# Attention and FFN in one kernel: ScalarE's Exp passes alternately two and three PSUM banks wide

## The chip, the cores and the metric

The kernel runs on one core of one Trainium2 chip. The metric is the device time of one execution in microseconds (us), as the median of the runs shown. A core has five engines with their own instruction queues, each running in order: TensorE (PE in the profile; its weight loads are PEld), VectorE (DVE), ScalarE (ACT), GpSimd (POOL) and SyncE (SP, which here only starts transfers). Matmul results land in PSUM. The kernel uses it as eight banks of 128 partitions by 512 float32 columns.

## The reference

For one sequence of S = 2048 tokens with D = 512 features, an attention block with 32 heads of width 16 and a SwiGLU FFN of inner width 1792 are computed from the same x, and mixed by a gate:

```python
g = sigmoid((x * gate_w).sum(-1, keepdims=True))
q, k, v = split_heads(x @ A_wqkv)                  # 32 heads of 16
p = softmax(q @ k.T * 16 ** -0.5)                  # 2048 x 2048 per head
a = merge_heads(p @ v) @ A_wo
b = (silu(x @ B_w_gate) * (x @ B_w_up)) @ B_w_down
out = g * a + (1 - g) * b
```

Inputs and output are bf16. The 32 x 2048 x 2048 = 134 million exponentials are the largest single item.

## The kernel before, in words

**Tiling.** Queries come in 4 blocks of 512 columns (`QB`, `QBW`), heads in 8 groups of four (`G`), keys in 16 tiles of 128 (`KT`). A *unit* is one query block with one head group; there are 32 (`UNITS`). A unit and a key tile make a *tile* of scores: four *blocks*, one for each head, of 128 keys by 512 queries. There are 512 tiles and 2048 blocks.

**Two ways to the exponential.** A tile goes one of two ways as a whole.
- On ScalarE: `emit_pair` (line 774) takes two blocks, has TensorE write their scores into `s_t`, a PSUM tile of two banks, and has ScalarE run one Exp over all 1024 columns into the SBUF tile `e_t` (line 793). Four blocks take two passes. Two `s_t` tiles exist, so one is filled while the other is read. Ten `e_t` buffers exist (`EB`).
- On VectorE and GpSimd: `emit_d` (line 855) writes one block into `d_t`, a single *shared* bank. VectorE turns the scores into the bits of an exponential with one TENSOR_SCALAR from PSUM to SBUF (`c_t<-d_t`; some tiles use spare space in `kaug` or `wd_t` instead). Then a tile is finished either with four shifted copies or with two masks and a product (`quad`, `groups`); VectorE runs these passes, and GpSimd takes strips of the columns of many of them.

Afterwards `pv` (line 1104) multiplies the exponentials by V into `o_ps`, one bank, accumulated over the whole unit. A column of ones in V also gives the softmax denominators.

**How score matmuls share TensorE.** A head's scores need only 32 of TensorE's 128 rows, so several blocks run side by side on different rows in one round. A `d_t` block *rides* along in the round of a pair, on the rows of heads that the pair does not use.

**PSUM.** Two `s_t` tiles (4 banks, `ps_s`), `o_ps` (1 bank, `ps_o`), and 3 shared banks (`ps_m`). The shared banks serve `d_t` and all other products: projections (`qp`, `kp`, `vp`), the FFN's `gu`, the output products `ops` and `dps`. A bank is taken by `m_tile` (line 396) and comes free once VectorE has emptied it (`m_free`).

**Order.** The whole program is straight-line; a planner fixes the order of the instructions while it is built. It keeps its own clocks for TensorE, VectorE, ScalarE and GpSimd (`plan.pe`, `plan.dve`, `plan.act`, `plan.pool`) with a price for each operation (`ACT_US` = 0.9167 for an Exp pass) and the times at which it expects the shared banks to be free (`banks`). The main loop (lines 1754 to 1814) fills the time until the next `s_t` tile is free with `pv` products or pieces of projections and FFN (`Chain`, `Pacer`, ordered by deadline), then emits the next pair. Where more than 0.4 us is left, it adds a filler product on `o_ps` with zero weights (line 1799). `want_d` (line 1741) says how many `d_t` blocks ride: at most as many as shared banks that the planner expects to be open at that moment, less one if another chain needs it:

```python
open_ = sum(b is not None and b <= max(plan.pe, s_end[pairs[0] % 2]) + (BANK_WAIT if way_of(pairs[0]) != "x" else 0.5) for b in banks)
...
return max(0, min(2, open_ - int(one), (3 if way_of(pairs[0]) != "y" else 4) - len(d_wait)))
```

`v_unit` (line 1700) chooses the unit whose last ScalarE tile is handed to VectorE instead. So how many tiles each engine gets is not written down; it comes out of these rules. On top of the rules, `TURNS` (line 88) is a string with two characters for each pass, read by `turn_of` and `way_of`: a letter at a place nudges one decision there.

**FFN.** Gate and up products of one 128-wide chunk are two chains of four pieces. `gate` (line 715) puts a Tanh, `th`, into ScalarE's queue between the passes; two VectorE passes follow. The weights of a chunk are loaded three chunks ahead into four buffers (`w_load`, `ffnw`).

**Head and tail.** Ahead of the loop, the first queries and six key tiles are projected and bounded (lines 1282 to 1366); the other ten key tiles follow under the first passes, and the queries are then computed again with the final bound (`q0_again`). After the loop the last unit's `o_ps` is copied in halves by ScalarE and VectorE, its denominators are inverted and spread over the rows, and four output tiles are finished with the last products of the output projection (`tail`, lines 1252 to 1268 and 1854 to 1887).

Of the kernel before, what the change touches and what calls it, by code (L numbers as in the profile page):

```python
# [54 lines left out]
class Pacer:  # L55
# [27 lines left out]

TURNS = (
    ".......u................g.a.k...............i...a................n.....x...v..s................."
    "j............x.x....e....g.......r.r.g....c.c...a......x..................e....r.w.....y........"  # L90
    "......hn.x..............j.h.........if.....v.......m........k.............i....q..........a....."
    "....h.o..........r.........f..f.h.........gt.....uhm............................................"
    "....................j................................qb..g.r.............x.................y...."
    "........k.d............g.f......f..o...............w................hf................k..t...r.."
    "..........s.........h........w...f........................s............................g........"
    ".......g.......v...y...r........k......o........c..............................................."
    ".....d..........i.a......lo..g......e..t..e..v.......r.........................................."
    "............a..m....f...i.k......rk........x.......lk.............k..........d...............g.."
    "..............b....y........o......w.....u..e..f.................r....b........................."
    "........................e................................u...m.........v..i........w.qcq.....w.."  # L100
    "bm.q..e.......c.......................................a..................u...w.w.......r..g....."
    ".................g.....................................................n..........h............."
    ".......wj.h...k....d.................................l....g......y......ov.n....i......l......k."
    ".n.........ls.g...i.......j.d....lb"
)
# [3 lines left out]
def kernel(  # L109
# [67 lines left out]
    ps_m = [ctx.enter_context(tc.tile_pool(name=f"ps_m{i}", bufs=1, space=bass.MemoryType.PSUM)) for i in range(3)]  # L177
# [150 lines left out]
    banks = [0.0] * 3  # L328
    held = [None] * 3
# [66 lines left out]
    def m_tile(name, ride=None):  # L396
        while m_ready() is None:
            stuck()
        i = min((i for i in range(3) if banks[i] is not None), key=lambda i: banks[i])
# [359 lines left out]
    def score(ps, b, rows=64):  # L759
# [3 lines left out]
        q = (q0a if n < FT else q0[qb])[r, j % 2, :] if g == 0 else get_q(qb, g)[r, j % 2, :]  # L763
        mm(ps, lhsT=kaug[r, g, kt * P:(kt + 1) * P], rhs=q, start=True, stop=True,
           tile_position=(r.start, 0))
# [8 lines left out]
    def emit_pair(bs, ride=0):  # L774
        i = pairs[0] % 2
        plan.pe = max(plan.pe + (FLIP if plan.mode != "R" else 0.0), s_end[i])
        if FT <= bs[0] // 4 < KT:
# [25 lines left out]

    def turn_of(n):

        return TURNS[2 * n] if 2 * n < len(TURNS) else "."

    def way_of(n):

        return TURNS[2 * n + 1] if 2 * n + 1 < len(TURNS) else "."  # L810

    exps = []
    ACT_US = 0.9167
# [9 lines left out]
    def d_slots(half=None):  # L823

        left = vcur["left"] if vcur else range(NV)
        return [k for k in left if half is None or k // 2 == half]
# [341 lines left out]
    def post(un):  # L1168
# [83 lines left out]
    def tail_ready():  # L1252
        for c in list(pace.chains):
            force(c)
        while owed:
            pay()
        assert here_done and len(scaled) == TQ
        al = ps_s.tile([P, 2 * QBW], F32, tag="s", name="al")
        a_ps.append(al)

    def tail(n):

        for _ in range(n):
            tq, i = rest.pop(0)
            if tq == 3 and i == 0:
                a_ps.append(ps_o.tile([P, QBW], F32, tag="o", name="al_o"))
            w, r = last_rows(tq)(i)
            mm(a_ps[tq][:, 0:D], lhsT=w, rhs=r, start=(i == 0), stop=False)

# [14 lines left out]
    def keep_warm(n):  # L1284
        for _ in range(n):
            mm(warm[:, :], lhsT=idle[:, 0:P], rhs=idle[:, :], start=True, stop=True)
# [27 lines left out]
    keep_warm(9)  # L1314
    for i0, i1, h in ((0, TQ, fore), (TQ, FT, aft)):
        for dc in (DC - 1, DC - 2):
            spare_s = dc < DC - 1 and i0
            p = ps_s.tile([P, 2 * QBW], F32, tag="s", name="tp") if spare_s else m_tile("tp")
# [6 lines left out]
            if not spare_s:  # L1325
                m_free(p, 0.0 if dc == DC - 1 else 0.1)
    pad(0)
    keep_warm(1)
    kpf = ps_s.tile([P, 2 * QBW], F32, tag="s", name="kp0")
# [19 lines left out]
    vp0 = m_tile("vp")  # L1349
    v0(vp0, 0, 0, 3)  # L1350
    for p, h in zip(qps, halves):
        bound_add(p[:, 0:HQ], kneg1, aq0[:, h])
    v0(vp0, 0, 3, FT)
# [11 lines left out]
    vec.tensor_copy(**v0_out(vp0, 0, FT))  # L1365
    m_free(vp0, plan.pe + 2.0)

    plan.act = plan.pe
    plan.dve = plan.pe + 2.3
# [7 lines left out]
    def k0_pieces(i, k0, w):  # L1377
# [14 lines left out]
        return columns(DC, "kp", lambda dc: wpad[1][:, dc, :], lambda dc: xT[:, dc, k0:k0 + w], end, c0)  # L1392

# [21 lines left out]
    def scale_part(p):  # L1415
        def f():
# [6 lines left out]
                        1, -101)  # L1423
    second = [pace.add(k0_pieces(2 + i, k0, min(QBW, S - k0)), 1, -100 + 0.1 * i)
              for i, k0 in enumerate(range(FK, S, QBW))]
    for a, c in zip([qp_again] + second, second):
        c.hold = lambda a=a: plan.pe >= 2.3 and a.out()
# [67 lines left out]
    def first_loads():  # L1495
        for i in range(3):
# [7 lines left out]
    for pos, qb in enumerate(ORDER):  # L1504
        a0 = f0 + per * pos
        gus = []
        for i in range(FC * pos, FC * pos + FC):
            gate_pcs, up_pcs = gu_chain(i)

            def first(f=gate_pcs[0][1], i=i):  # L1510
                w_load(i + 3, True)
                w_load(i + 3, False)
# [73 lines left out]
    def pv_list(now):  # L1586

        un = closed
        if un == UNITS or not o_ready(now):
            return []  # L1590
        early = un == 0 and pvs[0] < FT
# [16 lines left out]
    def emit_pv(item, most=QBW):  # L1608
        nonlocal closed
        un = closed  # L1610
        pv(item[0], item[1] if len(item) > 1 else None, most)
# [80 lines left out]
    LEAD, LAST = 8.0, 6.0  # L1692
    TILE_US = 1.9
# [6 lines left out]
    def v_unit():  # L1700
# [4 lines left out]
        while vu < UNITS:  # L1705
# [4 lines left out]
            left = hi[vu] - (at_ + max(half, begun) if vu == au else 0)  # L1710
            if vu >= au and left > 0 and (vu or hi[0] > FT):
# [41 lines left out]

    while au < UNITS:
# [10 lines left out]
        if room > 0.02:  # L1765
# [29 lines left out]
            if room > 0.4 and closed in o_of and 0 < pvs[closed] and pv_left(closed) > 1 and (closed or pvs[0] != FT) and sum(  # L1795
# [13 lines left out]
        begun = 1  # L1809
        emit_pair([4 * n + 2 * half, 4 * n + 2 * half + 1], want_d())  # L1810
        half ^= 1
        begun = 0
        at_ += not half
        forward()
    flush_act()
    while closed < UNITS or vops or vcur:
# [13 lines left out]
        if closed == UNITS - 1 and pv_left(closed) <= 2 and not a_ps[2:]:  # L1830
            tail_ready()
        if len(a_ps) > 2 and not pv_list(plan.pe) and not vops and len(rest) > 1:
            n = closed * KT + done_a[closed]
            if plan.pe + 0.22 < max(e_end.get(b, 0.0) for b in range(4 * n, 4 * n + 4)):
                tail(1)
                spend("F", 1)
                continue
        next_pv()
    for c in list(pace.chains):
# [5 lines left out]
    for n in sorted(at):  # L1845
        for f in at.pop(n):
            f()
    while jobs:
        oust()
    while owed:  # L1850
        pay()
    assert not vops and not vready and not vcur and not d_wait and not copies and au == closed == UNITS


    assert not at
    un = UNITS - 1
    osb = osbs[un]
    tail(min(2, len(rest)))
    dt = m_tile("dt")
    denominators(dt, osb)  # L1860
    rt = work.tile([P, 4 * TQ], BF16, tag="rt", name="rt")
    recip16(rt[:, :], dt[:, 0:4 * TQ])
    tail(sum(r[0] == 2 for r in rest))
    spread_rows(dt, rt, (0,), P)
# [54 lines left out]
```

## Time and profile before

| what | value |
|---|---|
| median of the runs | 743.07 us (2 runs, 742.9 to 743.23) |
| profiled execution: its own time | 742.59 us |
| its span, first to last instruction | 740.9 us |
| granted TensorE clock | 0.999 |
| matmuls; VectorE; ScalarE; GpSimd instructions | 9224; 1227; 827; 362 |
| Exp passes of 1024 columns | 754 |
| `th` passes of 512 columns | 56 |
| `d_t` blocks (into `c_t`, `kaug` and `wd_t`) | 468 + 60 + 12 = 540 |

Columns of a row of instruction groups: line, engine, operation, output<-input, shapes, count, then after the bar the busy time in us, the mean length of one instruction in ns, and the idle time of that engine just before them with what ended it. Instructions of one engine may overlap, so busy time is less than count times mean. A row of the table by stage has the stretch, its length, and each engine's busy time with the number of instructions.

### The profile page before, as it was taken

Reading aid. Unit: us, or ns where it says so; the run is one execution under the profiler, and the core shown is the slowest. Engines: PE = TensorE matmul, PEld = TensorE weight load, DVE = VectorE, ACT = ScalarE, POOL = GpSimd, SP = SyncE. Lnnn points to the kernel's source line nnn. Section 1 sums busy time; section 2 is a strip of 40 time slices with the busy share of each in tenths; the row PEclk is TensorE's granted clock in tenths of the full one; section 3 lists DMA queues with packets and bytes.
Section 4 is the critical chain, followed back from the end, with each engine's and each line's share of the span. In section 5 each row is a group of like instructions: output and inputs, shape, how many; then the busy total and the mean of one; then the engine's idle time right before and its main releaser. Section 6 shows DMA issues by size and latency. Waiting matters only on the chain.

```text
span 740.9 us, 22996 instructions
## 1 busy us (share of the span) xinstructions
PE 722.7 (98%) x9224; PEld 212.8 (29%) x9225; DVE 717.8 (97%) x1227; ACT 727.7 (98%) x827; POOL 286.6 (39%) x362
## 2 busy tenths in 40 slices
PE   8999999999999999999999999999999999999997
PEld 3323223232222222322222222222222322222222
DVE  5999999999999999999999999999999999999996
ACT  7999999999999999999999999999999999999995
POOL 4044242234353336345444224544234244443320
PEclk9999999999999999999999999999999999999999
DMA  9001233345220012320200041302001232100001
GB/s 227 10 2 30 57 60 61 62 119 117 71 48 13 18 42 68 72 48 11 57 18 24 15 106 34 78 23 58 18 23 31 51 81 58 32 19 13 25 22 36
DMA packets 93523, 36.29 MB, mean 49 GB/s; under 512 B 76448, under 2 KB 92968, under 8 KB 93416
## 3 DMA queue, kind: packets, MB, share of 16 engines
q1 hardware_dynamic: 91688, 34.49, 19.9%
q8 instruction: 72, 1.18, 0.6%
q10 hardware_dynamic: 1728, 0.33, 0.2%
q14 instruction: 35, 0.29, 0.1%
HBM read 21.42 MB, written 2.35 MB: 32 GB/s over the span
## 4 chain that ended last, share of the span: by engine, by line
PE 57%; ACT 29%; issue 7%; DVE 6%; SPq 0%; DMA 0%; ACTq 0%; DVEq 0%
ACT e_t L197 27%; PE s_t L194 20%; PE o_ps L194 17%; PE gu L194 7%; PE ops L194 6%; DVE c_t L206 3%; ACT th L197 2%; PE qp L194 2%; PE vp L194 2%; PE kp L194 1%; PE dps L194 1%; DVE mt L206 1%; DVE kaug L206 1%; PE warm L194 1%; SPq L206 0%
## 5 line engine op out<-in xcount | busy, mean ns | idle before, releaser
L197 ACT ACTIVATE e_t<-s_t 128x1024 bf16<-128x1024 f32 x754 | 704.2, 1101 | 0.4 <-PE s_t L194 0.2
L206 DVE TENSOR_SCALAR c_t<-d_t 128x512 uint16<-128x512 f32 x468 | 306.4, 679 | 2.9 <-PE d_t L194 2.3
L206 POOL TENSOR_SCALAR c_t<-c_t 128x352 uint16<-128x352 uint16 (+19 forms) x216 | 154.3, 715 | 233.1 <-DVE c_t L206 147.8
L194 PE MATMUL s_t<-qx,kaug 32*128 32x512 bf16 (+1 forms) x1200 | 233.4, 384 | 9.9 <-ACT e_t L197 8.5
L194 PEld LDWEIGHTS <-kaug 32*128 32x128 bf16 (+1 forms) x2048 | 80.7, 91 | 311.5 <-issue 308.5
L194 PE MATMUL d_t<-qx,kaug 32*128 32x512 bf16 x440 | 152.6, 384 | 0.0
L194 PE MATMUL o_ps<-e_t,vaug 128*32 128x512 bf16 (+1 forms) x1588 | 148.3, 375 | 0.0
L194 PE MATMUL o_ps<-c_t,vaug 128*32 128x512 bf16 (+2 forms) x1392 | 124.4, 375 | 0.1
L206 DVE TENSOR_SCALAR c_t<-c_t 128x2048 uint16<-128x2048 uint16 (+8 forms) x187 | 116.8, 635 | 0.4
L206 POOL TENSOR_TENSOR c_t<-c_t 128x480 bf16<-128x480 bf16 (+7 forms) x46 | 56.7, 1240 | 108.7 <-DVE c_t L206 74.6
L194 PEld LDWEIGHTS <-vaug 128*32 128x32 bf16 x3212 | 66.7, 95 | 104.8 <-issue 94.2
L194 PE MATMUL gu<-xT,wg 128*32 128x512 bf16 x896 | 72.2, 384 | 0.0
L194 PE MATMUL gu<-xT,wu 128*32 128x512 bf16 x896 | 65.9, 382 | 0.3 <-DVE kaug L206 0.2
L194 PE MATMUL ops<-wd_t,mt 128*32 128x512 bf16 x672 | 57.0, 382 | 0.0
L206 DVE TENSOR_TENSOR c_t<-c_t 128x1568 bf16<-128x1568 bf16 (+7 forms) x46 | 43.9, 954 | 0.0
L206 DVE SCALAR_TENSOR_TENSOR gs<-th,gu 128x512 bf16<-128x512 bf16 x56 | 37.9, 677 | 1.5 <-ACT th L197 1.4
L206 DVE TENSOR_SCALAR kaug<-d_t 128x512 uint16<-128x512 f32 x60 | 39.3, 678 | 0.1
L206 DVE SCALAR_TENSOR_TENSOR mt<-gs,gu 128x512 bf16<-128x512 bf16 x56 | 37.8, 675 | 0.7 <-PE gu L194 0.5
L197 ACT ACTIVATE th<-gu 128x512 bf16<-128x512 f32 x56 | 38.2, 682 | 0.0
L194 PE MATMUL s_t<-q,kaug 32*128 32x512 bf16 (+1 forms) x184 | 35.8, 385 | 1.0 <-ACT e_t L197 0.9
L194 PEld LDWEIGHTS <-mt 128*32 128x32 bf16 (+1 forms) x1058 | 25.0, 95 | 28.2 <-issue 21.9
L206 DVE TENSOR_SCALAR kaug<-c_t 128x2048 uint16<-128x2048 uint16 (+3 forms) x44 | 29.3, 666 | 0.0
(152 smaller groups left out, 543.4 us busy)
## 6 DMA issues: line engine op xcount, KB each, us to landing
wg<-in_B_w_gate_dram SPq DMA_DIRECT2D x56, 128.0 KB
wu<-in_B_w_up_dram SPq DMA_DIRECT2D x56, 128.0 KB
on<-osb SPq DMA_DIRECT2D x120, 16.0 KB
rb<-rr SPq DMA_DIRECT2D x15, 128.0 KB
kaug<-kbt SPq DMA_DIRECT2D x28, 64.0 KB
wd_t<-in_B_w_down_dram SPq DMA_DIRECT2D x7, 256.0 KB
qx<-qst SPq DMA_DIRECT2D x96, 16.0 KB
qx<-aq SPq DMA_DIRECT2D x96, 16.0 KB
```

Source lines behind the costliest of these rows:

```text
L194: return ordered(nc.tensor.matmul(*args, **kw))
L197: ordered(nc.scalar.activation(*args, **kw))
L206: return lambda *a, **kw: ordered(f(*a, **kw))
```

## The change

`s_t` is no longer one kind of tile: two pools make one tile of two banks and one of three, used in turn. Two shared banks are left instead of three. `emit_pair` now takes two or three blocks, which may cross the border of a key tile or a unit (`next_banks`). The Exp buffers come in the same two widths, five of each. The planner counts 0.9167 us for a two-bank pass and `BANK_US` = 0.3657 more for the third bank.

```diff
-TURNS = (... 16 lines ...)
+NUDGE = ""
...
-    etp = ctx.enter_context(tc.tile_pool(name="etp", bufs=EB))
+    etp = ctx.enter_context(tc.tile_pool(name="etp", bufs=1))
-    ffnw = ctx.enter_context(tc.tile_pool(name="ffnw", bufs=4))
-    opool = ctx.enter_context(tc.tile_pool(name="opool", bufs=2))
+    ffnw = ctx.enter_context(tc.tile_pool(name="ffnw", bufs=3))
+    opool = ctx.enter_context(tc.tile_pool(name="opool", bufs=1))
-    ps_s = ctx.enter_context(tc.tile_pool(name="ps_s", bufs=2, space=bass.MemoryType.PSUM))
+    ps_s = [ctx.enter_context(tc.tile_pool(name=f"ps_s{i}", bufs=1, space=bass.MemoryType.PSUM)) for i in range(2)]
-    ps_m = [... for i in range(3)]
+    ps_m = [... for i in range(2)]
+    S_BANKS = (2, 3)
+    def s_tile(i, name):
+        return ps_s[i].tile([P, S_BANKS[i] * QBW], F32, tag=f"s{i}", name=name)
+    def e_tile(i):
+        return etp.tile([P, S_BANKS[i] * QBW], BF16, tag=f"e{i}", name="e_t", bufs=EB // 2)
...
     def emit_pair(bs, ride=0):
...
-        ride = d_slots(1 - bs[0] % 4 // 2)[:ride]
-        s_t = ps_s.tile([P, 2 * QBW], F32, tag="s", name="s_t")
-        e_t = etp.tile([P, 2 * QBW], BF16, tag="e", name="e_t")
+        ride = d_slots([k for k in range(NV) if all(b % 4 != k for b in bs)])[:ride]
+        s_t, e_t = s_tile(i, "s_t"), e_tile(i)
+        w = len(bs) * QBW
         for k, b in enumerate(bs):
-            score(s_t[:, k * QBW:(k + 1) * QBW], b, 32 if ride else 64)
+            score(s_t[:, k * QBW:(k + 1) * QBW], b, 32 if ride or len(bs) > 2 else 64)
...
         def exp():
-            act(out=e_t[:], in_=s_t[:], func=ACT.Exp, scale=inv_sqrt_dh)
-            plan.act = max(plan.act, ready) + ACT_US
+            act(out=e_t[:, 0:w], in_=s_t[:, 0:w], func=ACT.Exp, scale=inv_sqrt_dh)
+            plan.act = max(plan.act, ready) + ACT_US + BANK_US * (len(bs) - 2)
...
-    ACT_US = 0.9167
+    ACT_US, BANK_US = 0.9167, 0.3657
...
-    LEAD, LAST = 8.0, 6.0
-    TILE_US = 1.9
+    LEAD, LAST = 8.0, 7.0
+    TILE_US = 1.83
...
+    def next_banks(m):
+        u, t, p, r = au, at_, half, []
+        while len(r) < m:
+            if p == 0 and t == hi[u]:
+                u, t = u + 1, 0
+            if u == UNITS - 1 and hi[u] - t <= KF or r and p == 0 and (u, t) == (0, FT):
+                break
+            r.append(4 * (u * KT + t) + p)
+            p += 1
+            if p == 4:
+                t, p = t + 1, 0
+        return r, (u, t, p), ...
...
-        emit_pair([4 * n + 2 * half, 4 * n + 2 * half + 1], want_d())
+            bs, to, begun = next_banks(S_BANKS[pairs[0] % 2])
+            emit_pair(bs, want_d())
```

Four further edits go with it.
- *Nudges.* With `NUDGE` empty, `turn_of` and `way_of` always give ".", so only the rules order the program.
- *FFN weights* are loaded two chunks ahead into three buffers, and one output buffer is left instead of two.
- *Head.* Three of the first six V tiles (`v_begin`) and the repeated projection of the first queries (`qp_again`) move behind the first passes and the second keys; some tiles of the head use `ps_o` or `ps_s` instead of a shared bank.
- *Tail.* The last two key tiles on ScalarE (`KF` = 2) are taken by halves of the query columns: two passes with 256 columns of each of four heads for the first half, then two for the second (`emit_fin`, `pv_fin`). VectorE copies each half of `o_ps` (`fin_copy`), and a list of steps with the planner's costs (`step`) orders what is left, the second half (output tiles 2 and 3) and the first (0 and 1) each with its own denominators and spreading. Before, ScalarE copied one half.

```diff
-        elif un == UNITS - 1:
-            o = o_of.pop(un)
-            act(out=osbs[un][:, 0:HQ], in_=o[:, 0:HQ], func=ACT.Identity, bias=tiny[:, 0:1], scale=1.0)
-            vec.tensor_scalar(out=osbs[un][:, HQ:QBW], in0=o[:, HQ:QBW], scalar1=TINY, scalar2=None, op0=ALU.add)
...
+    def emit_fin():
+        i, f = pairs[0] % 2, len(fin_e)
+        n, h = fin[f]
...
+        for k in range(4):
+            score(s_t[:, fin_cols(k)], 4 * n + k, 64, slice(h * HQ, h * HQ + HQ))
...
+            act(out=e_t[:, 0:2 * QBW], in_=s_t[:, 0:2 * QBW], func=ACT.Exp, scale=inv_sqrt_dh)
```

More of the change, by code (lines that the diff above doesn't have):

```diff
@@ L327 @@
     work_at = []
-    banks = [0.0] * 3
-    held = [None] * 3
+    banks = [0.0] * 2
+    held = [None] * 2
     def spend(mode, mms, ready=0.0):
@@ L398, in m_tile @@
             stuck()
-        i = min((i for i in range(3) if banks[i] is not None), key=lambda i: banks[i])
+        i = min((i for i in range(2) if banks[i] is not None), key=lambda i: banks[i])
         if ride is None:
@@ L757, with score @@
     HEADS = (0, 2, 1, 3)
-    def score(ps, b, rows=64):
+    def score(ps, b, rows=64, cols=slice(0, QBW)):
         n, j = b // 4, HEADS[b % 4]
@@ L821, with d_slots @@
     y_live = [0]
-    def d_slots(half=None):
+    def d_slots(heads=range(NV)):
         left = vcur["left"] if vcur else range(NV)
-        return [k for k in left if half is None or k // 2 == half]
+        return [k for k in left if k in heads]
     users = {}
@@ L1250 @@
     rest = [(tq, i) for tq in (2, 3) for i in range(NB + 3 - tq)]
[L1252 to L1268, printed above, removed]
     def out_pieces(qb, tq):
@@ L1392, in k0_pieces, with v_first, f, end @@
         return columns(DC, "kp", lambda dc: wpad[1][:, dc, :], lambda dc: xT[:, dc, k0:k0 + w], end, c0)
+    def v_first(i):
+        def f():
+            v0(vp0, 0, i, i + 1)
+            spend("F", 0.8)
+            if i == FT - 1:
+                later(0.6, end)
+        def end():
+            vec.tensor_copy(**v0_out(vp0, 0, FT))
+            o_end[0] = plan.dve + 0.1
+            for t in range(FT):
+                v_at[t] = plan.dve + 0.1
+        return f
+    for t in range(FT):
+        v_at[t] = 1e9
+    v_begin = pace.add([(0.8, v_first(i), False, "F", None) for i in range(V0, FT)], 0, -103)
+    need[2] = [v_begin]
     known_at = []
@@ L1495, in first_loads @@
     def first_loads():
-        for i in range(3):
+        for i in range(2):
             w_load(i, True)
@@ L1590, in pv_list @@
             return []
+        if un == UNITS - 1 and pv_left(un) == KF:
+            f = fin_done[0]
+            return [("f",)] if f < min(KF, len(fin_end)) and (now is None or fin_end[f] <= now) else []
         early = un == 0 and pvs[0] < FT
@@ L1610, in emit_pv @@
         un = closed
+        if item[0] == "f":
+            pv_fin()
+            return
         pv(item[0], item[1] if len(item) > 1 else None, most)
@@ L1808 @@
         n = au * KT + at_
-        begun = 1
-        emit_pair([4 * n + 2 * half, 4 * n + 2 * half + 1], want_d())
-        half ^= 1
+        if au == UNITS - 1 and not fin and not half and hi[au] - at_ <= KF:
+            while vcur:
+                lone_d()
+            fin.extend((n + f % KF, f // KF) for f in range(2 * KF))
+            osbs[au] = work.tile([P, QBW], BF16, tag="osb", name="osb")
+        if fin:
+            begun = 1
+            emit_fin()
+            half ^= 1
+            at_ += not half
+        else:
+            bs, to, begun = next_banks(S_BANKS[pairs[0] % 2])
+            emit_pair(bs, want_d())
+            au, at_, half = to
         begun = 0
-        at_ += not half
         forward()
     flush_act()
-    while closed < UNITS or vops or vcur:
+    while closed < UNITS - 1 or fin_done[0] < KF or vops or vcur:
         fill_dve()
@@ L1829 @@
             continue
[L1830 to L1837, printed above, removed]
         next_pv()
+    begin(SLOTS + 1)
     for c in list(pace.chains):
@@ L1844, with fin_dens, fin_inv, fin_spread @@
         pay()
[L1845 to L1864, printed above, removed]
-    rps = ps_s.tile([P, 2 * QBW], F32, tag="s", name="rps")
-    spread_rows(rps, rt, range(1, TQ))
-    on_l = work.tile([P, QBW], BF16, tag="rd", name="on_l")
-    for tq in range(TQ):
-        cs = slice(tq * P, (tq + 1) * P)
-        vec.tensor_tensor(out=on_l[:, cs], in0=osb[:, cs], in1=rps[:, cs] if tq else dt[:, P:2 * P], op=ALU.mult)
-    for tq in (0, 1, 3, 2):
-        tail(min(1, len(rest)) if tq < 2 else len(rest))
+    assert not vready and not d_wait and not copies and au == UNITS and not at
+    assert here_done and len(scaled) == TQ
+    older = pairs[0] % 2
+    a_ps.append(s_tile(1 - older, "al"))
+    fin_l = {}
+    on_l = work.tile([P, QBW], BF16, tag="rd", name="on_l")
+    osb = osbs[UNITS - 1]
+    def fin_dens(h):
+        p = s_tile(older, "dt") if h == 0 else ps_o.tile([P, QBW], F32, tag="o", name="dt")
+        fin_l["p", h] = p
+        for tq in (2 * h, 2 * h + 1):
+            mm(p[:, 4 * tq:4 * tq + 4], lhsT=osb[:, tq * P:(tq + 1) * P], rhs=sel_t[:, :], start=True, stop=True)
+    def fin_inv(h):
+        rt = work.tile([P, 4 * TQ], BF16, tag="rt", name="rt")
+        recip16(rt[:, 8 * h:8 * h + 8], fin_l["p", h][:, 8 * h:8 * h + 8])
+        fin_l["r", h] = rt
+    def fin_spread(h):
+        spread_rows(fin_l["p", h], fin_l["r", h], (2 * h, 2 * h + 1), P - 2 * P * h)
+    def fin_norm(tq):
+        cs, c0 = slice(tq * P, (tq + 1) * P), P + tq % 2 * P
+        vec.tensor_tensor(out=on_l[:, cs], in0=osb[:, cs], in1=fin_l["p", tq // 2][:, c0:c0 + P], op=ALU.mult)
+    def fin_product(tq):
         mm(a_ps[tq][:, 0:D], lhsT=on_l[:, tq * P:(tq + 1) * P], rhs=wo_l[:, 1, :], start=False, stop=True,
            skip_group_check=tq < 2)
-    for tq in range(TQ):
+    left = {"out": 2}
+    def fin_out(tq):
         t = (QB - 1) * TQ + tq
@@ new lines, with step @@
+    steps = {}
+    def step(name, engine, cost, f, *after):
+        steps[name] = (engine, cost, f, after)
+    for f in range(KF, 2 * KF):
+        step(("v", f), "C", 0.55, pv_fin, (f - 1 if f > KF else "os0", 0.0), (("e", f), 0.0))
+    step("os1", "V", 0.42, lambda: fin_copy(1), (("v", 2 * KF - 1), 0.25))
+    step("dt1", "F", 0.5, lambda: fin_dens(1), ("os1", 0.06))
+    step("rc1", "V", 0.22, lambda: fin_inv(1), ("dt1", 0.25))
+    step("sp1", "C", 1.5, lambda: fin_spread(1), ("rc1", 0.3))
@@ new lines @@
+    for tq in (2, 3, 0, 1):
+        step(("c", tq), "V" if tq % 2 else "A", 0.74 if tq % 2 else 0.69, lambda tq=tq: fin_out(tq), (("p", tq), 0.25))
+    while len(fin_end) < 2 * KF:
+        flush_act()
+    over = {("e", f): t for f, t in enumerate(fin_end)}
+    over.update({f: plan.pe for f in range(KF)})
+    over["os0"], over["s"] = fin_osb[0], s_end[older]
+    al_at = lambda tq: over.get(("n", 1), 1e9) + 0.06 if tq == 3 else s_end[1 - older]
+    now = {"V": plan.dve, "A": plan.act}
+    while steps:
+        best = None
+        for name, (engine, cost, f, after) in steps.items():
+            if all(a in over for a, t in after):
+                start = max([now.get(engine, plan.pe)] + [over[a] + t for a, t in after])
+                if best is None or start < best[0] - 0.02:
+                    best = start, name
+        lim = min([max(plan.pe, max(over[a] + t for a, t in st[3])) for st in steps.values() if st[0] in "CF" and all(a in over for a, t in st[3])], default=1e9)
+        if rest and not (best and best[0] <= plan.pe) and plan.pe + 0.12 <= lim and max(plan.pe, al_at(rest[0][0])) + 0.12 <= min(lim, 1e8):
+            tq, i = rest.pop(0)
+            if tq == 3 and i == 0:
+                a_ps.append(s_tile(older, "al_o"))
+            w, r = last_rows(tq)(i)
+            mm(a_ps[tq][:, 0:D], lhsT=w, rhs=r, start=(i == 0), stop=False)
+            spend("F", 1, al_at(tq))
+            if not rest or rest[0][0] != tq:
+                over["l", tq] = plan.pe
+            continue
+        start, name = best
+        engine, cost, f, after = steps.pop(name)
+        if engine in "CF":
+            if name[0] == "v":
+                plan.pe = max(plan.pe, start)
+                f()
+                over[name[1]] = plan.pe
+            else:
+                f()
+                spend(engine, cost, start)
+            over[name] = plan.pe
+        else:
+            plan.dve = start
+            f()
+            now[engine] = over[name] = start + cost
+            plan.dve = now["V"]
@@ L1892 @@
+    plan.pe = max(now.values())
+    un = UNITS - 1
+    osb = osbs[un]
 _INS = ['A_x', 'A_wqkv', 'A_wo', 'B_x', 'B_w_gate', 'B_w_up', 'B_w_down', 'gate_w']
```

130 lines of the change are left out of this document (82 added, 48 removed).

## The prediction

> **What bounds the kernel now.** I read the page first: its busy shares, the slices, the chain that ended last and the costliest groups.
>
> ```profile
> PE 722.7 (98%) x9224; PEld 212.8 (29%) x9225; DVE 717.8 (97%) x1227; ACT 727.7 (98%) x827; POOL 286.6 (39%) x362
> ...
> PE 57%; ACT 29%; issue 7%; DVE 6%; SPq 0%; DMA 0%; ACTq 0%; DVEq 0%
> ...
> L197 ACT ACTIVATE e_t<-s_t 128x1024 bf16<-128x1024 f32 x754 | 704.2, 1101 | 0.4 <-PE s_t L194 0.2
> L206 DVE TENSOR_SCALAR c_t<-d_t 128x512 uint16<-128x512 f32 x468 | 306.4, 679 | 2.9 <-PE d_t L194 2.3
> L206 POOL TENSOR_SCALAR c_t<-c_t 128x352 uint16<-128x352 uint16 (+19 forms) x216 | 154.3, 715 | 233.1 <-DVE c_t L206 147.8
> ```
>
> Three engines are full at once. That is balance, not three separate bounds: the kernel gives each block of 128x512 scores either to ScalarE (Exp) or to VectorE with GpSimd (the bit trick on `d_t`). So the question about the change is how many blocks ScalarE gets and what one costs there. The table of busy time by stage shows that ScalarE hardly stops between its first and last Exp pass.
>
> ```profile
> core 0: us, PE busy (x) PEld busy (x) DVE busy (x) ACT busy (x) POOL busy (x), PEclk, DMA share, GB/s
> 0.00:10.48 10.48, 8.85 (x72) 4.75 (x72) 5.35 (x32) 5.35 (x13) 7.93 (x22) 1.00 0.89 187
> ...
> 200.00:300.00 100.00, 98.60 (x1276) 27.70 (x1277) 99.60 (x166) 100.00 (x114) 44.60 (x57) 1.00 0.16 39
> ...
> 500.00:600.00 100.00, 99.85 (x1298) 28.17 (x1298) 99.47 (x163) 99.94 (x114) 36.22 (x48) 1.00 0.18 45
> ...
> 731.20:740.90 9.70, 5.29 (x50) 1.83 (x47) 3.68 (x9) 1.85 (x3) 0.00 (x0) 0.91 0.20 68
> ```
>
> The span is therefore 10.48 us of head, 720.7 us in which ScalarE runs passes end to end (10.48 to 731.18), and 9.7 us of tail. The timeline of ScalarE gives the price of a pass; columns are start, length, engine, operation.
>
> ```profile
> 444.38 0.59 ACT L197 ACTIVATE th<-gu 128x512 bf16<-128x512 f32 x1
> 444.85 4.70 ACT L197 ACTIVATE e_t<-s_t 128x1024 bf16<-128x1024 f32 x5
> 449.37 0.67 ACT L197 ACTIVATE th<-gu 128x512 bf16<-128x512 f32 x1
> 449.85 5.69 ACT L197 ACTIVATE e_t<-s_t 128x1024 bf16<-128x1024 f32 x6
> ```
>
> Passes overlap, so starts count, not lengths. From 444.85 to 449.37 five passes of 1024 columns take 4.52: 0.904 each, the floor. The 512-wide `th` holds the engine from 449.37 to 449.85: 0.48 (0.476 read to the nanosecond). Doubling the columns thus costs 0.4275, and what a pass costs beside its columns is only 0.476 - 0.4275 = 0.05 us. Over the whole stage, 720.7 less 56 x 0.476 for `th` and 0.6 for two small ones, over 754, is 0.920 a pass: 0.016 above the floor is waiting.
>
> **The change, part by part.** *Wider passes.* A three-bank pass was never run here. Its price is 0.904 plus a third bank. Bounds for that bank: 0.384 below (the only 512-wide Exp, `mt<-mt`, starts at 27.92 and the next pass at 28.44, so 0.52 for 512; 0.904 - 0.52) and 0.460 above (half of the mean 0.920, as if nothing were saved). I take 0.4275, whose two rows are both backed-up PSUM reads: 1.331 for 1536 columns. Merging saves about 0.05 us for each pass that disappears. At an unchanged 1508 blocks, alternating widths would make 603 passes of 754 and save 151 x 0.05 = 8 us at best.
>
> The Trainium skill, "ScalarE: Activation LUTs", section "What ACT_TABLE_LOAD costs", gives 186 ns plus 0.833 ns a column for a pass with immediate operands, and 93 ns of overlap. By it a pass would cost 0.946 and 1.373 us here and a saved pass 93 ns; the slope agrees with the rows (0.4267 a bank), the fixed part (0.05 measured) does not. By the page the same programs would have 713 us of Exp before and 796 us after.
>
> *Who gets the blocks.* The instruction lists of the two built programs settle what the diff hides. Before: 754 passes of two banks (1508 blocks) and 540 `d_t` blocks. After: 348 passes of 1024 and 340 of 1536, so 696 + 1020 = 1716 blocks on ScalarE and 332 `d_t` blocks; both make 2048. Passes fall by only 66, worth 66 x 0.05 = 3 us, while ScalarE takes 208 more blocks at 0.4275: +89 us. The rule that does it is `want_d`: a VectorE block rides along with a score round only into a shared bank that is open at that moment, and only on a head that the pass does not use. There are two shared banks where there were three, and a three-bank pass leaves one head free where a pair left two.
>
> *The sum for ScalarE.* At the floor: 348 x 0.904 + 340 x 1.331 = 767.1; with `th` and the small ones (27.3) 794.4. I add 0.002 of waiting a pass, not the 0.016 of before, giving 795.8: ScalarE will be the only full engine, so its queue of ready score tiles stays filled. Against 720.7 that is +75.1. With all of the old waiting it would be 805.
>
> *VectorE, GpSimd, TensorE.* VectorE loses 208 evictions of `d_t` at 0.679 (-141), 32 copies and masks at some 0.64 (-20, from the row of 0.635) and 67 products at 0.954 (-64); 718 - 225 is 493 us of 815, or 60%. GpSimd falls from 362 to 127 instructions. TensorE has 9216 matmuls for 9224 with 8% more time. All this is relief off the path; it buys nothing unless ScalarE waits for it. The filler products on `o_ps` (32 groups of four) cost nothing for the same reason: they fill idle TensorE time, and at 0.22 a group would be 7 us if they did not.
>
> *Two shared banks elsewhere.* About 520 tiles, for some 720 before, go through two banks instead of three. Each is held for its matmul and a VectorE eviction of 0.68. A wait there is hidden as long as it is shorter than the Exp pass running beside it (0.90 or 1.33). I take zero; unhidden, half a microsecond at each of the 56 gate/up pairs would be 28 us.
>
> *Queues and buffers.* Weights of the FFN are fetched two chunks ahead instead of three. The chunk distance in the busy stretch is about 5 us (`th` at 444.38 and 449.37), so two ahead is about 10 us for loads whose issue takes 0.46 us on SyncE; no wait for them shows on TensorE before. One output buffer instead of two is used 12 times between 378 and 731 us, so it is free again long before. SyncE has 612 instructions in both. Ten Exp buffers stay ten, half of them wider.
>
> *Head and tail.* The head still evaluates the same 24 first blocks; three of six V tiles move behind the first passes, and the repeat projection behind the second keys. These hold two shared banks, so the switch to the second queries (near 20 us) can be late by 0 to 2.5 us; the head's start can gain up to 0.4. I take zero for both together. In the tail, the last four passes are two key tiles by half the columns, so the first half's copy of `o_ps` is over before the last Exp ends. Before, the last Exp ended at 731.18 and the copy of the second half at 733.82, 2.6 us later. After, the last half-width products (0.35), their lag (0.25) and the 256-column copy (0.42) need about 1.3. What follows (reciprocal, spreading, products, output) has the same length, with tile 3 now last on TensorE, about +0.3. Tail 8.7 instead of 9.7; bounds 7.6 and 10.2.
>
> *Order by rules alone.* The nudge string is emptied. What the nudges did to waiting is inside the 0.016 a pass above.
>
> **Sum.** 10.5 + 795.8 + 8.7 = 815.0 us of span. Before, span 740.9 belongs to an execution of 742.6, so 1.7 lies around it: 816.7. The median shown is 743.07, 0.5 above that execution: 817. That is 10% slower.
>
> **The rivals.** *R1, the third bank is cheaper.* The changed code itself counts 0.3657 us a bank (`BANK_US`), below the lower row. Then 340 x (0.4275 - 0.3657) = 21 us less: 796. Against it stands the floor: with 0.3657 a bank, `th` would cost 0.904 - 0.366 = 0.54, and it costs 0.476.
>
> *R2, ScalarE starves.* TensorE runs in order; held for a shared bank, it brings the next scores late, and `th`, which sits in ScalarE's queue among the passes, waits for its gate product. At 0.5 us for each of 56 pairs: 845. For it: two banks, and every gate/up pair needs one each. Against it: VectorE, which empties them, is 40% idle after, and the cover of 0.9 to 1.3 us is longer than an eviction.
>
> *R3, not slower: the spacing is a handoff, not columns.* If 0.904 were the round of ScalarE freeing a tile and TensorE refilling it (0.39 for the matmul, plus semaphores), a 1536-wide pass would also take about 0.904, ScalarE would need 688 x 0.906 + 27 = 650, and the old 720 to 723 us of TensorE would set the end: about 742, no change. It decides once the third bank costs under 0.25 (within 2%: 817 - 758 = 59, over 340 is 0.17 below 0.4275). Against it: passes overlap (1.02 to 1.15 long at 0.904 spacing), their wait for `s_t` is 0.4 us in all, and `th` shows that time follows columns.
>
> **How the numbers follow.** Forecast 0.74, R1 0.10, R2 0.13, R3 0.03. The third bank's bounds move the time by 340 x (-0.044 to +0.033), that is -15 to +11; the old waiting would add 10, the head and tail -1.5 to +4. From 801 to 834 the range takes in these bounds, in all their likely combinations, and a mild R2; R1 at its full size, R2 at its full size and R3 stay outside, some 2 in 10. A measurement of this kernel tells about 2% from no change: faster 0.01, same 0.02, slower 0.97.
>
> **What would show it.** Right: two Exp groups, x348 spaced about 0.905 and x340 about 1.33; ACT near 98% busy and first in the chain; DVE near 60%, POOL near 14%; last Exp ends near 806. R1: wide passes spaced near 1.27. R2: idle time of ACT before `e_t` or `th`, released by PE, over 15 us. Wrong altogether: DVE still above 90%, or wide passes under 1.16.

## The result and the profile after

The changed kernel takes 827.5 us against 743.07: a ratio of 1.1135, 95% interval 1.1117 to 1.1154. It is 11% slower; 817 was predicted, in a range of 801 to 834. The profiled execution took 826.46 us with a span of 824.7.

The page after, engines first (busy us, share, instructions), then the chain that ended last, then three groups of instructions:

```profile
PE 720.2 (87%) x9217; PEld 248.6 (30%) x9217; DVE 546.0 (66%) x918; ACT 811.1 (98%) x760; POOL 81.1 (10%) x122
...
ACT 61%; issue 20%; PE 15%; DVE 1%; SPq 1%; DMA 0%; ACTq 0%; DVEq 0%
...
L183 ACT ACTIVATE e_t<-s_t 128x1024 bf16<-128x1024 f32 (+1 forms) x688 | 796.7, 1451 | 2.3 <-PE s_t L180 2.0
L192 DVE TENSOR_SCALAR c_t<-d_t 128x512 uint16<-128x512 f32 x284 | 194.8, 688 | 134.7 <-PE d_t L180 133.1
L180 PE MATMUL s_t<-qx,kaug 32*128 32x512 bf16 (+2 forms) x1380 | 216.8, 381 | 73.0 <-ACT e_t L183 70.0
```

The balance is gone. ScalarE alone stays full at 98% and leads the chain (61%, before 29%). VectorE falls to 66%, GpSimd to 10%. TensorE stands still in front of its score matmuls (73 us in this group) until Exp frees the tile. VectorE stands still 133 us in front of `c_t<-d_t`, because no block has come.

The busy time by stage, cut at the first and the last Exp pass:

```profile
0.00:10.57 10.57, 8.32 (x60) 4.09 (x60) 5.35 (x32) 5.34 (x12) 7.94 (x22) 1.00 0.91 182
10.57:817.12 806.55, 707.79 (x9120) 242.91 (x9121) 537.49 (x878) 804.46 (x746) 73.18 (x100) 1.00 0.18 42
817.12:824.70 7.58, 4.08 (x43) 1.55 (x41) 3.13 (x9) 1.27 (x3) 0.00 (x0) 0.93 0.21 69
```

Head 10.57 (before 10.48), Exp stage 806.55 (720.7), tail 7.58 (9.7). The whole loss, +85.9, lies in the stage; the tail gives back 2.1. And ScalarE's timeline after:

```profile
315.29 0.86 ACT L183 ACTIVATE th<-gu 128x512 bf16<-128x512 f32 x1
315.77 5.82 ACT L183 ACTIVATE e_t<-s_t 128x1024 bf16<-128x1024 f32 x5
321.30 0.77 ACT L183 ACTIVATE th<-gu 128x512 bf16<-128x512 f32 x1
321.78 10.68 ACT L183 ACTIVATE e_t<-s_t 128x1536 bf16<-128x1536 f32 x9
332.09 0.86 ACT L183 ACTIVATE th<-gu 128x512 bf16<-128x512 f32 x1
```

A row here merges both widths and shows that of its first pass. Read to the nanosecond, the shortest spacing in the stage is 0.904 behind a narrow pass, 1.330 behind a wide one and 0.477 behind `th`: 0.427 for each 512 columns and 0.05 beside them. The rows fit: from 321.78 to 332.09 five wide and four narrow passes take 10.31 (5 x 1.330 + 4 x 0.904 = 10.27); from 315.77 to 321.30 three narrow and two wide take 5.53 (5.37). What is over, 0.04 and 0.16, is waiting.

### The profile page after: what moved, and what is told of

Its sections match the earlier page's. It is cut to its first block, busy times and chain, and to the rows that moved or that the text cites. A ratio compares the mean times of both kernels' runs of the same rounds, so it can differ in the third digit from the quotient of the medians.

```text
span 824.7 us, 22164 instructions
## 1 busy us (share of the span) xinstructions
PE 720.2 (87%) x9217; PEld 248.6 (30%) x9217; DVE 546.0 (66%) x918; ACT 811.1 (98%) x760; POOL 81.1 (10%) x122
## 4 chain that ended last, share of the span: by engine, by line
ACT 61%; issue 20%; PE 15%; DVE 1%; SPq 1%; DMA 0%; ACTq 0%; DVEq 0%
ACT e_t L183 57%; PE s_t L180 5%; ACT th L183 4%; PE gu L180 3%; PE o_ps L180 3%; SPq L192 1%; PE qp L180 1%; DVE c_t L192 1%; DMA xT<-in_A_x_dram 0%; PE kp L180 0%; PE ops L180 0%; DVE mt L192 0%; PE vp L180 0%; PE a_l_a L180 0%; PE al L180 0%
## 5 line engine op out<-in xcount | busy, mean ns | idle before, releaser
L183 ACT ACTIVATE e_t<-s_t 128x1024 bf16<-128x1024 f32 (+1 forms) x688 | 796.7, 1451 | 2.3 <-PE s_t L180 2.0
L192 DVE TENSOR_SCALAR c_t<-d_t 128x512 uint16<-128x512 f32 x284 | 194.8, 688 | 134.7 <-PE d_t L180 133.1
L180 PE MATMUL s_t<-qx,kaug 32*128 32x512 bf16 (+2 forms) x1380 | 216.8, 381 | 73.0 <-ACT e_t L183 70.0
L180 PE MATMUL o_ps<-e_t,vaug 128*32 128x512 bf16 (+3 forms) x1752 | 166.3, 381 | 0.0
L192 DVE TENSOR_SCALAR c_t<-c_t 128x2048 uint16<-128x2048 uint16 (+6 forms) x168 | 103.3, 645 | 2.7
L180 PE MATMUL d_t<-qx,kaug 32*128 32x512 bf16 x268 | 102.7, 385 | 0.0
L180 PEld LDWEIGHTS <-vaug 128*32 128x32 bf16 (+1 forms) x3196 | 68.2, 94 | 113.2 <-issue 97.5
L180 PE MATMUL o_ps<-c_t,vaug 128*32 128x512 bf16 (+2 forms) x1124 | 96.9, 375 | 1.8 <-DVE osb L192 1.6
L192 POOL TENSOR_SCALAR c_t<-c_t 128x352 uint16<-128x352 uint16 (+9 forms) x57 | 38.7, 679 | 406.8 <-DVE c_t L192 255.3
L192 DVE SCALAR_TENSOR_TENSOR mt<-gs,gu 128x512 bf16<-128x512 bf16 x56 | 38.4, 685 | 19.5 <-PE gu L180 18.2
L180 PEld LDWEIGHTS <-wu 128*32 128x32 bf16 x896 | 21.0, 95 | 26.1 <-issue 15.3
L192 DVE TENSOR_SCALAR osb<-o_ps 128x512 bf16<-128x512 f32 (+1 forms) x32 | 21.4, 668 | 9.2 <-PE o_ps L180 7.7
```

Source lines behind the costliest of these rows:

```text
L180: return ordered(nc.tensor.matmul(*args, **kw))
L183: ordered(nc.scalar.activation(*args, **kw))
L192: return lambda *a, **kw: ordered(f(*a, **kw))
```

## The experiments

Theory D (division): two shared banks let fewer blocks ride to VectorE, the rest goes to ScalarE at 0.427 a block, and ScalarE sets the end. Rivals: W, the wide passes themselves cost; N, the lost nudges cost; S, ScalarE is starved because TensorE is held at a shared bank; H, the spacing of passes is a handoff that hides columns. Theory L came up on the way: weights two chunks ahead are late. In the table, "floor" is passes times their shortest spacing (0.9035, 1.3305) plus 27.3 for `th` and two small ones; "waits" is the stage less the floor; all times in us. The kernel before stands at 743.0 in these comparisons.

| kernel | Exp passes | VectorE blocks | floor | stage | waits | tail | median |
|---|---|---|---|---|---|---|---|
| before | 754 | 540 | 708.5 | 720.7 | 12.2 | 9.7 | 743.0 |
| nudges emptied | 770 | 508 | 723.0 | 735.8 | 12.8 | 8.7 | 756.8 |
| new head and tail, 2+2 banks, 3 shared, weights 3 ahead | 768 | 512 | 721.2 | 741.4 | 20.2 | 9.6 | 763.3 |
| the same, 2 shared | 844 | 360 | 789.9 | 811.3 | 21.4 | 7.7 | 832.8 |
| changed kernel (2+3 banks, 2 shared, weights 2 ahead) | 348 + 340 wide | 332 | 794.1 | 806.6 | 12.5 | 7.6 | 827.5 |

**1. Only the wide tile undone** (`e1_two_wide`).

```diff
-    S_BANKS = (2, 3)
+    S_BANKS = (2, 2)
```

> The changed kernel with both score tiles two banks wide again, two shared banks kept (one bank unused). The instruction lists: 844 Exp passes of 1024, 360 blocks on VectorE. Theory D (division: two shared banks let fewer blocks ride to VectorE, and ScalarE sets the end): 844 x 0.9035 + 27.3 = 789.9, waiting 844 x 0.017 = 14, head and tail 18.2, 1.7 around: 824, within 1% of the changed kernel. Rival W (the three-bank pass is what costs): back to 745 to 760.

Measured: 842.0, ratio to before 1.1331 (1.1309 to 1.1354). W is out: without wide passes it is no faster. But D missed by 18. ScalarE lost 11.2 and 3.4 us at two places. Here is the first, in the timeline of all engines:

```profile
162.07 4.96 SPq L192 DMA_DIRECT2D qx<-aq  x8
167.12 0.53 SPq L192 DMA_DIRECT2D wd_t<-in_B_w_down_dram  x1
167.75 0.41 SPq L192 DMA_DIRECT2D wg<-in_B_w_gate_dram  x1
...
170.52 1.47 PE L180 MATMUL gu<-xT,wg 128*32 128x512 bf16 x12 [10.12 <-DMA wg<-in_B_w_gate_dram]
...
172.63 1.02 ACT L183 ACTIVATE e_t<-s_t 128x1024 bf16<-128x1024 f32 x1 [10.84 <-PE s_t L180]
```

The brackets hold the idle time before and what ended it. TensorE waits 10.1 us for gate weights, and ScalarE behind it 10.8 for scores. The weights were issued only at 167.75, because SyncE had 24 small transfers in front (`kaug<-kbt`, `qx<-qst`, `qx<-aq`, 149.5 to 167.0 in its own timeline). Two chunks ahead are about 10 us; the queue was 17.5 us long. That is theory L, and the changed kernel itself escapes it: its weight loads wait 0.7 us for `wg` in all.

**2. Two-bank tiles and the third shared bank back** (`e2_three_shared`).

```diff
-    S_BANKS = (2, 3)
+    S_BANKS = (2, 2)
-    ps_m = [... for i in range(2)]
+    ps_m = [... for i in range(3)]
```

> As the previous one, and the third shared bank given back; nudges still empty, new head, tail and buffers kept. The instruction lists: 768 Exp passes of 1024, 512 blocks on VectorE. Theory D: 768 x 0.9035 + 27.3 = 721.2, waiting 13, head and tail 18.2, 1.7 around: 754; so this one bank takes away some 70 of the 84 us. Rival N (loss of the nudges): stays above 800. Rival W: same as the kernel with two shared banks.

Measured: 776.3, ratio 1.0444 (1.0413 to 1.0476). One bank is worth 66 us against experiment 1, close to D's 70; the level is 22 too high. TensorE waited 10.1 us for gate weights and 4.6 for the first key weights in the head.

**3. The kernel before with its nudges emptied** (`e3_no_nudges`).

```diff
-TURNS = (... 16 lines ...)
+TURNS = ""
```

> The kernel before with its string of nudges emptied and nothing else. The instruction lists: 770 Exp passes, 508 blocks on VectorE. Theory D: 16 passes more at 0.92 = +14.7, so 758. Rival N: most of the 84 us, above 800. If the nudges only removed waiting, ScalarE's mean pass would grow beyond 0.925 as well.

Measured: 756.8, ratio 1.0189 (1.0175 to 1.0203). N is a sixth of the loss. The waits do not grow (12.2 to 12.8): the nudges are worth what they bring to VectorE, 32 blocks.

**4. The kernel before with the new tail only** (`e4_new_tail`): the changed code of the loop's end and after it, in the kernel before with all its nudges.

```diff
+        if fin:
+            emit_fin()
...
+        step(("v", f), "C", 0.55, pv_fin, ...)
```

> The kernel before with its nudges and three shared banks, and only the tail of the changed kernel (last two key tiles by halves of the columns). The instruction lists: 754 passes and 540 blocks as before. If the tail of the changed kernel is worth what its profile shows (7.6 us after the last Exp instead of 9.7), 741.0, 0.28% faster than before. If the shorter tail came only from engines that had less to do there, 743.

Measured: 742.1, ratio 0.999 (0.9981 to 0.9999). The tail shrinks from 9.7 to 9.0, not to 7.6. So the new tail alone gives a third of what the changed kernel shows. That the rest comes from engines with less left to do is not shown: the same tail code takes 9.6 us in experiment 6 and 7.7 in experiment 5, which differ by one shared bank, but 15.3 and 9.1 in experiments 9 and 10, again with two shared banks. This is the only version that beat the kernel before, by 0.1%; the interval ends at 0.9999.

**5 and 6. Theory L tried: weights three chunks ahead again**, in experiments 1 and 2.

```diff
-    ffnw = ctx.enter_context(tc.tile_pool(name="ffnw", bufs=3))
+    ffnw = ctx.enter_context(tc.tile_pool(name="ffnw", bufs=4))
-                w_load(i + 2, True)
-                w_load(i + 2, False)
+                w_load(i + 3, True)
+                w_load(i + 3, False)
```

(and three chunks in `first_loads`). With two shared banks (`e9_two_wide_w3`):

> The changed kernel with two-bank tiles only, two shared banks, and the FFN weights again three chunks ahead in four buffers. Same lists of passes as with two chunks ahead: 844 passes, 360 blocks on VectorE. Theory D with theory L (weights two chunks ahead land late once SyncE's queue is held up): the 16 us that ScalarE lost to two late weight loads go, 842 - 16 = 826, within 0.5% of the changed kernel. If the late weights were an accident of that program's order and not of the depth: 835 to 842.

With three (`e10_three_shared_w3`):

> The same with three shared banks: 768 passes, 512 blocks. Theories D and L: the 776 measured with two chunks ahead less the 10 to 12 us that TensorE waited for weights: 765; what stays above the 754 of the bare sum is the head's wait for the key weights (5.3) and a longer tail. Theory D alone: 776.

Measured: 832.8, ratio 1.1215 (1.1194 to 1.1235), and 763.3, ratio 1.0274 (1.0258 to 1.0289). The depth matters: 9.2 and 13.0 us. The first lies between its two forecasts, 826 and 835 or more: one late load remains, for which TensorE waits 5.6 us, so three ahead is not always enough either. The second lies 2 below its forecast. Of its 9 us above the bare sum of 754, the longer tail makes 2, and most of the rest is one line of TensorE's waits (total, times, longest):

```profile
PE kp L180 <- DMA wqk<-in_A_wqkv_dram: 5.3, 1, 5.3
```

It waits for the first key weights in the head. Neither experiment 3 (old head, three shared banks) nor the changed kernel (new head, two) has this wait, so it takes the new head together with three shared banks; why is open.

These two differ in the number of shared banks alone, and give the price of the bank: 69.6 us. Each holds one wait for a load that costs ScalarE 6.1 us, so these two cancel. Their groups of `d_t` evictions into `c_t`, two shared banks first, then three:

```profile
L192 DVE TENSOR_SCALAR c_t<-d_t 128x512 uint16<-128x512 f32 x308 | 210.6, 688 | 138.0 <-PE d_t L180 136.7
```

```profile
L192 DVE TENSOR_SCALAR c_t<-d_t 128x512 uint16<-128x512 f32 x444 | 292.2, 683 | 14.0 <-PE d_t L180 13.3
```

With the bank gone, VectorE's idle time in front of these evictions rises from 14 to 138 us: it is not slower, it is not fed. The floors differ by 68.7 us (844 against 768 passes), the waits by 1.2. So nearly all of the price is division and almost none starvation: D holds, S falls.

**7. A third bank for nothing** (`e5_free_third`).

```diff
-            act(out=e_t[:, 0:w], in_=s_t[:, 0:w], func=ACT.Exp, scale=inv_sqrt_dh)
+            act(out=e_t[:, 0:min(w, 2 * QBW)], in_=s_t[:, 0:min(w, 2 * QBW)], func=ACT.Exp, scale=inv_sqrt_dh)
...
-            e_of[b] = e_t[:, k * QBW:(k + 1) * QBW]
+            e_of[b] = e_t[:, min(k, 1) * QBW:(min(k, 1) + 1) * QBW]
```

> The changed kernel, but each three-bank pass reads and writes only its first 1024 columns (the second block's exponentials stand in for the third's); TensorE's, VectorE's and GpSimd's instructions are unchanged. Theory D: ScalarE needs 688 x 0.9035 + 27 = 649 and stops being the bound; TensorE, which stood waiting for Exp 88 us of 825, then sets the end: 740 to 755, about the kernel before. So even a free third bank would not beat it. Rival S (ScalarE is starved at shared banks): TensorE's waits stay, above 800. Rival H (spacing is a handoff): no change, 827.

Measured: 753.3, ratio 1.0137 (1.0117 to 1.0156).

```profile
PE 712.4 (95%) x9217; PEld 224.4 (30%) x9217; DVE 540.7 (72%) x918; ACT 694.3 (93%) x760; POOL 80.8 (11%) x122
...
PE 71%; DVE 13%; ACT 8%; issue 4%; DMA 2%; SPq 1%; DVEq 0%; ACTq 0%
```

340 x 0.427 = 145 us were taken from ScalarE, and 74 came out at the end; then TensorE leads the chain (71%, in the changed kernel 15%). H is out (time follows columns), and S again: with less Exp, TensorE kept up a faster pace through the same two shared banks. It also bounds the idea behind the change: with this order of TensorE's work and this division, even a free third bank does not reach the kernel before.

**8. The wide pass split in two** (`e6_split`).

```diff
-            act(out=e_t[:, 0:w], in_=s_t[:, 0:w], func=ACT.Exp, scale=inv_sqrt_dh)
+            for c0, c1 in [(0, min(w, 2 * QBW))] + [(2 * QBW, w)] * (len(bs) > 2):
+                act(out=e_t[:, c0:c1], in_=s_t[:, c0:c1], func=ACT.Exp, scale=inv_sqrt_dh)
```

> The changed kernel with each three-bank pass split into one of 1024 and one of 512 columns; the same columns, 340 passes more. Theory D by the rows: 340 x 0.05 = +17, so 844. If widening a pass saves more than the rows say (0.093 a pass): 859. Rival P (columns of a third bank are dearer than 0.4275): less than +17, down to 827.

Measured: 850.2, ratio 1.1442 (1.1421 to 1.1462): +22.7 on the changed kernel. A 1024 pass with its 512 rest takes 0.915 + 0.478 = 1.393 on average, a wide pass 1.339: 0.054 for each pass saved, 18 us over 340, as the rows said. The other 5 us are longer waits behind the other 1024 passes (0.946 on average instead of 0.928). Rival P is out: columns of a third bank are not dearer.

**9. The rule that lets a block ride, loosened** (`e7_wait`).

```diff
-    BANK_WAIT = 0.2
+    BANK_WAIT = 0.6
```

> The changed kernel with one constant changed: a block may ride if a shared bank is expected open within 0.6 us instead of 0.2 (BANK_WAIT). The instruction lists: 338 passes of 1024 and 332 of 1536, 376 blocks on VectorE. Theory D: 44 blocks less on ScalarE, 338 x 0.9035 + 332 x 1.3305 + 27.3 = 774.4, waiting 12, head and tail 18.2, 1.7 around: 806, 21 less than the changed kernel. Rival S (TensorE held at a shared bank starves ScalarE): the longer waits eat the gain, 820 or more.

Measured: 821.8, ratio 1.1051 (1.103 to 1.1071); 6 us better, not 21. The floor fell by 19.7 as counted. The stage fell by 12.6 only, since the waits of ScalarE rose from 12.5 to 19.5. The longest of them, which costs 3.1, is theory L again, weights that come late:

```profile
509.69 1.04 PE L180 MATMUL gu<-xT,wg 128*32 128x512 bf16 x8 [2.54 <-DMA wg<-in_B_w_gate_dram]
...
511.38 1.45 ACT L183 ACTIVATE e_t<-s_t 128x1536 bf16<-128x1536 f32 x1 [2.68 <-PE d_t L180]
```

The other 4 us fit S, at a fifth of the gain: TensorE's waits in front of `gu` for VectorE's `gs` rose from 1.8 to 4.9 us. The tail took another 7.7:

```profile
ACT mt L183 <- PE a_l_a L180: 10.3, 1, 10.3
```

This line of ScalarE's waits (total, times, longest) is its wait after the last Exp, 2.6 in the changed kernel. When the last Exp ends, TensorE still has 72 products of other output tiles (`ops`, until 808.7) ahead of the last unit's.

**10. The planner's price of a third bank corrected** (`e8_price`).

```diff
-    ACT_US, BANK_US = 0.9167, 0.3657
+    ACT_US, BANK_US = 0.9167, 0.4275
```

> The changed kernel with the planner's price of a third bank set to the measured 0.4275 instead of 0.3657. The instruction lists: 344 passes of 1024 and 336 of 1536, 352 blocks on VectorE. Theory D: 785.2, waiting 12, head and tail 18.2, 1.7 around: 817, 10 less. If the wrong price also caused the waits of a wide pass behind a narrow one (7.5 us in the changed kernel), 812. If the division is not what sets the time: 827.

Measured: 821.2, ratio 1.1055 (1.1038 to 1.1071): 6 us better; 10 was expected. The profiled stage falls by 6.2 for a floor lower by 8.9. The waits of a wide pass behind a narrow one do not go away (10.5 us, before 7.5), so the wrong price is not what keeps them.

**Put together**, by medians: nudges +13.8 (experiment 3); new head, tail and buffers +6.4 (763.3 less 756.8); the third shared bank +69.6; wide passes with weights two ahead -5.3 (827.5 less 832.8). The sum is 84.5. By the floors alone the same four steps are +14.5, -1.8, +68.7 and +4.2, or 85.6 of the 85.9 us that the stage lost, while the waits are 12.2 before and 12.5 after. So the division accounts for the whole loss of the stage. The +6.4 is mostly the 6.1 us that experiment 6 loses to its key weights, a wait that the changed kernel does not have. The -5.3 is no gain of wide passes: the floor rises by 4.2 (794.1 less 789.9), as 28 more blocks at 0.427 (12 us) outweigh 156 passes saved at 0.05 (8 us); the waits fall by 9, of which 6.1 is the one late weight load of the kernel compared. Two things were not run: the nudges taken away with two shared banks in place of three, and nudges made anew for the changed kernel.

## Why the prediction was right, step by step

- *Who gets the blocks* carried it. 208 blocks more on ScalarE at 0.4275 = 89 us, less 3 for passes saved, against +85.9 measured in the stage. The named rule (`want_d`, open shared banks) is the cause: experiments 5 and 6 give 152 of the 208 blocks to the bank, experiment 3 gives 32 to the nudges, experiment 1 gives 28 to the wide pass; the new head, tail and buffers give back 4. Experiment 9, which loosens this rule and nothing else, moves 44 blocks back to VectorE. That the 28 come from the single free head was not tested apart.
- *The price of a pass.* 1.331 predicted, 1.330 the shortest, 1.339 the mean. R1 is out.
- *Waiting* was the step that failed in size. "I add 0.002 of waiting a pass, not the 0.016 of before" put 1.4 us into the stage; measured are 12.5, or 0.018 a pass. The reason given, that a full ScalarE keeps its queue filled, was wrong: 66 of 310 narrow passes were followed by a wide one more than 0.03 late (6.5 us; 7.5 over all 310), but none of 312 wide passes by a narrow one. The refill of the wide tile has only the narrow pass, 0.904, to hide behind, that of the narrow tile 1.331. The trace bears this out: 60 of the 66 start 0.10 to 0.11 us after the end that it gives for their own score matmuls, so they wait for scores. In 39 of them (1.9 us) TensorE had begun these matmuls 0.05 us after the wide tile came free, so the refill of 0.39 us did not fit. In the other 27 (4.6 us) TensorE began them 0.09 to 1.0 us after the tile came free and had no idle time in front of them, so other products made it late; held at a bank, as in R2, it would have stood idle. No run removes either part by itself. Another 1.4 us lie at 20.7 us, where the scores wait for the second queries (TensorE waits 1.2 for `qx`); the text had bounds of 0 to 2.5 for that and took zero. With the old waiting the text had 805 for the stage, near the 806.6 measured; that this agrees so well is partly luck, as these waits are made up differently from the old ones.
- *Tail*: 8.7 predicted, 7.6 measured. The copy after the last Exp was over after 0.84 us, not 1.3; the three terms that the text names add up to 1.02. Experiment 4 shows that in the kernel before two thirds of this gain are not there.
- *VectorE* at 66% instead of 60%. The instructions went as counted: their lengths fell by 221 us in sum, 225 predicted. But lengths overlap, and the text took them off the busy time, where overlaps count once: the lengths sum to 807 us before and 586 after, the busy time is 718 and 546. GpSimd is at 10% instead of 14%. TensorE is off the path as said, 88 us waiting for Exp; its "8% more time" was 10% by the text's own sum.
- *Weights two chunks ahead at zero* held in this kernel, but by luck of its order: in experiments 1 and 2 the same depth cost 9 and 13 us. The prediction compared 10 us of lead with the 0.46 us of one issue, and did not count what can stand in front in SyncE's queue.
- *R2* did not happen here at the size it was given: ScalarE is idle ahead of its Exp passes for 2.3 us, and the sign was over 15. In experiment 9 some 4 of the 15 us that are missing fit it.
- *The price by the page*, the Trainium skill's "ScalarE: Activation LUTs", section "What ACT_TABLE_LOAD costs": its slope agrees with the runs (0.427 a bank); a merged pass saves 0.054 here (experiment 8), not the 0.093 that the prediction estimated from it.

## What to carry to other kernels

Before widening an instruction, find what it costs beside its columns: the spacing of two widths that run back to back gives it, and here it was 0.05 us of 0.904. A buffer that is given up for it can be what feeds another engine: count from the built program how the work is divided before and after, because 208 moved blocks decided this and no line of the diff names them. And a prefetch depth is to be held against the longest run of transfers ahead in the same queue, not against the time of one issue.

## What the runs showed of the hardware that was not expected

- Much of the spacing of ScalarE's passes falls on two steps 0.017 apart. Before, 429 of 695 spacings between Exp passes are 0.903 or 0.904 and 114 are 0.920; after, 160 of the 312 from a wide pass to a narrow one are 1.330 or 1.331 and 143 are 1.347 or 1.348. What selects the step stayed open; behind the wide passes it is about 2.6 us of the waits in the changed kernel.
- The recorded length of an Exp pass is no price: the mean length rose from 1.101 to 1.241 us for 1024 columns between the two profiles while the shortest spacing stayed 0.904.
